# A state-space convolution beside a gathered expert layer: a half-width step tile, ScalarE's phase results written 128 bytes apart, one more slot for gathered rows

## The chip, the cores and the metric

The kernel runs on one core of a Trainium2 chip. The metric is the device time of one execution in microseconds (us). A core has five engines that run their own instruction queues and wait for each other through semaphores: PE multiplies matrices, DVE does elementwise work, ACT evaluates functions, POOL here mostly starts gathers, SP starts the plain DMAs. All DMAs share 16 DMA engines.

## The reference

The input `x` has 2048 rows of 448 numbers. It is normalised by row (`xn`), and three things are added: `x` itself, a state-space convolution of `xn` along the rows, and an expert layer on `xn`.

```
A = A_re + i A_im;  dt = exp(log_dt)
P = exp(dt * A * l)                      # l = 0 .. 2047, for 448 channels x 256 modes
K = real(sum over modes of C * P * dt*B) # one filter of 2048 taps per channel
y = conv(xn, K) + xn * Dskip             # by FFT in the reference
q = xn @ w_q;  s1 = q1 @ k1.T;  s2 = q2 @ k2.T     # 16 heads, 64 scores each
e = argmax(s1) * 64 + argmax(s2)                    # one of 4096 experts per head
out = sum over heads of gelu(xn . u[e]) * v[e]
result = x + y + out
```

The gate `g` is a softmax over one element.

## The kernel before

**Filter.** The 448 channels are taken in 56 batches of 8, with 2 x 128 modes a batch. Complex powers of each mode are built from a magnitude and a phase. The phase is an integer, of which the full range is one turn, so that it wraps by itself. On each of 128 partitions a batch has 32 phases (exponents) for each of 32 columns, which are its 8 channels for two halves of the modes and two base steps `h`; the names call a column a mode `m`. They are built for two batches at a time in `s.ph`, by doubling. The first row is copied from the loaded phases (`row(-1)`), and four adds (`row(0)` to `row(3)`, L614) double the number of rows, 1, 2, 4, 8, to 16; each adds a step that is the base step shifted left. The shifted steps of four batches lie in the step tile `st`, made by `sh` in `steps` with two shifts (L547), one per half `h`; there are 14 such tiles. In this version a row holds each phase for two neighbouring exponents `x` side by side, so the step tile holds each step twice. The integer add is a custom DVE instruction and appears in the profile as CUSTOM_DVE_ANT_0 on halves of 16 bits.

ScalarE then reads the phases through the view `four`: `trig` (L629) takes the sine, `trig2` (L632) the absolute value, and `trig3` (L635) the sine of a quarter turn less that, which is the cosine. The result `CS` is ordered by mode, and within a mode by the 32 exponents. `four` reads two neighbouring integers, then jumps 512 bytes; the writes are one run. DVE multiplies magnitude `mg` by `CS` (L660 to L666, tile `zi` and `mg`), PE sums over modes (`kp`, L682) and transforms (`vp`, L702), and ACT evicts to `VK` (L706).

**Convolution.** The channels are cut in chunks of 128, 128, 128 and 64. For each chunk PE transforms (`U`, L798 or L779), DVE multiplies (L808 or L786), PE transforms back (`ip`), the result goes through DRAM (`t_d`), and `final` makes the last transform and adds the rows to the output by an accumulating DMA on POOL (L1167).

**Experts.** `combine` multiplies keys and query weights once (`wc`, L862), so that the scores are one product per tile of 128 rows (L961, L970). DVE finds the two winners, their numbers `ig` go through DRAM, and for each of 16 tiles and 4 groups POOL starts 4 indirect gathers of 128 rows of 3584 bytes (L1083, 256 in all), a row being `u` and `v` of an expert. DVE takes the dot product (L1091), ACT and DVE make the gelu, PE sums with a masked weight (L1121), and the tile is added to the output (L1136).

**Slots.** Gathered rows, the loaded rows `xx`, the combined weights `W` and the convolution's big tiles share one pool of slots of 4 KB per partition: `UE` + 4 + 7 + 3, with `UE` = 11. A gather waits until the slot that it is given has been read for the last time. POOL's DMA descriptors have an area of 4096 bytes of each partition.

**Order.** The kernel is written as steps in some fifty streams (a stream is one kind of step, such as gathers or phase adds). The string `ORDER` names, character by character, the stream whose next step comes; it sets the sequence of every engine's instructions and the sequence in which slots are taken and given back. Waits between engines follow from what a step reads and writes. `Plan.run` checks that no step comes ahead of what it needs.

Of the kernel before, what the change touches and what calls it, by code (L numbers as in the profile page):

```python
# [85 lines left out]
def dv(n, k=1.0):  # L86
    return (66 + n / k) / 0.96
# [28 lines left out]
class Plan:  # L116
# [61 lines left out]
    "zUIygU!#ISh!h#yyyISRzKRVROizWx$W$%yyfziHHhNgxSfSzxPxKLISiz!#JM#RjRLRSfI!$$%QzIhhgTJfiIziGISSzMfykI!#yIyU#RUi&hRhh!yI$S$i"
    "dIeRXUSzUO%jhSIUNSlizIIhPkhLRhQzISMLhTMyRdiLzibURe!yyRzMfUzlyUiU##NY!U$$%LShSgJRjyRZZSifMhKhgHzz!UzKxiHfSfaN#Ufyy(LJ!Skh"
    "M#$hOPgUzxUiSL$%RRSyhhyymzxHTMhmlizxUUSRhhhn!nhHjhkhgLMURiUSLhhUyz#gRyRQV1iziSIiNI!fiIzz!ifSYclmISfhM#fQ$I$%hnSSgO#IyTWf"  # L180
    "IiUzjhiKZPhHI!&hRmUIhR#QkW$UhnI$UyyyyUzIzlzU%!hHjRy#z!iziS#Iy$RS$hkJyyyL%ZiUSzzHHdMhyRyLMelIbROzISz!I#!Iy#$SygiPfIhiSSXm"
    "zfzhRJmRUfRU$%L!nITnjhgfi#SIUIfMLhIhMkUIUiSgRRR#h!ISli$$N%OIJjKxcNJhzxyyVhhcyyxSzzSyUySUxzSzh!TPi#h!h#QmULUWZ$aih&Kyyhnf"
    "$UfURfU%MRziSzUgyzyLhNMhRgifSLfRQz!hSiH(yhg#HWzz#h!$R$hhbjZzz%Riyh!k#y!#MHYO$SSd$%iyHPIhekSizIIUSzlliIiRRLjhIKQghTzIUiSh"
    "UIR!#UihISMkhKyIyyfI!UI#URlmyS$I$fURfSShnJVY%NcgROhKxhfSajXxUizzyyPiSxzgLkhyymRQixzz!M#z#N!$Rhym$lhzfinyL&%RTSyzy(njUSUz"
    "hUz!yhhgzhzMU#Uhk!!SWR##il$$fh!Ri%R#hzhJfyi$yzfyxz$OzyfgxSxxS%KfimSiSiUhhP!gL#RMRhjhL#TiUiyUWSd!z$hRUSyzRMR$yy%yhkhSiyhS"
    "izUnjzhkilSROUNY(Qzlh!zhSzUPy&#!y#ymiSR$z$egyUb%hny!h#!aRyzTizfzUgzSfyyRURSXfiUR#$NQSU$UROzUihSSxoz!xYhgmzSf%yzSyP#h#Uy!"
    "h!hyfURRjnhTiRkhhS$U#hyS$y%UiymjUzilk!#UlxV$$xg%&hzzz!zzWh#!(Sn#hRSyyzyiz!iyyRmRS#V#$Wh!my$$inno$fUoyfigSSph%hzfgp%zfzUq"
    "rzqzyyphYj!hhzUrizfiyTkqpqroz#rhhhi#!!dpjqlW#$hrebiUh#kst$!hpg%pqWhxh$iorfoo$qltUxpgypyfzrhqxhciXfUg%irszijhUyifq&pzfrUi"
    "yhkhyyxy(zlzU!thozy#p#!qzz$hy$pjq!hr##iy!z$cay%yhhiyg$yUzfyUhzfqhrzhkpz%qr!pyyygUVzrtWihhuqppl#zfzyghrfi#!hy!ms(#fd#$yqm"
    "hyu!hr$%nqteth$ii$irnyiymjYbxxmhxsihnkxKnhjii%tzhWilgfhhYt&ykzgzzQffzzzz!yhhgh#if#yy!l$fmmh!$#h#!izz%iji$ynhyyuhnhyzkhhl"  # L190
    "z$zzihjgfhzi!hf#z!kayfli#gfifib$ih!hg$mhhuhijd%#hi)heh)(ym!nini#*ki$ljhxzXm%i+hhkf$xzxlxngh%hmgyyyizzifi&f!ynhhjgyy#yyhh"
    "i!khflf#zh$h*$y+hjmnkhca%hzziiilmnYyzg!hiz#y!hhzzyf#$zjgh$chzfykg%yh!zfzfifihdhzl#!hmi#i!eh##nh)o*+jb$i$!i$hg$ihk,%%ix)x"
    "lhhyh*zfmjx+niiyYygykhhyzff,aiyyyzyilgyxy,,yXyzzf!h&zhjmyfklgnz#o#h!zmyhy!n$$p#p!#hhhhqzhq$%zih$izpzizifr%jqprzhpgqrifzf"
    "ypqkhrfhrifqpYrcgh!hhsploihqh#ijritq#!ztk!rhpphqis#olxhbr$iq$frtptpd%qiz#fi!qehghpjhigkx$rqhuayr$xph%fgzyy(qyxyYfliurpzp"
    "zrhsfyhqh!hqhhrmttum#!ijhrhisi#nknhghhyziyyz$zz!$fyizf&fgtht%mhlzf#!i#giynhhmjhknfi$izdehhhzlmn!$huhjghhhykb(yg#yyy)iii#"
    "!%zfxzzfzx!$$al#h!hgfxy#ymyhyhifinchjx)*%yi$ykfiijhh$khh%z+hhlgizlzzhhyiim!nzzzi)yfizf#f#iy!$igjh(yyyy!&hg$fh%#hyk!*ydiz"
    "zlzz#f$$zzzzhmn*+hyhhh,+hbhiijykmni%e!gfilh)xfxo*hgi+f#i!!hihi##!$jg#ff$$,hxz$chkh%lzhyh%hyxzjaoYgizik!iilhyz#y,yyyhfyjh"
    "z#zfh!hgyzk!i$f$lym#y#h!y,yyyymnhgif$iz$hhnmdzizfjzzhnhemkhzzlizhbiixh&%yh!nhi#i!gh!hm%g#iniijhh(#j!fy#kf$k$fxlghhm%xfyh"
    "z$fl$oxhm%nnhhzpqhgp&pyy(yzziihz!rqiihqyzpr#!h#ajhqpi$f$zi%gyfrzhopq!rf#h#frgph!hzfiz$qhkrspl$%hqiripyzhhtqhyy(yytzbjgrq"
    "ziyphsqhhhzfyrfgpi!ktpthhyyyfgrqqi#uxypfrh!hzhyqprszfqho!ihi#ii$$hl#jthzhr!#if$rut%kpfjlgvhhxfiihgpqhfxh$igq%khrifrohxou"  # L200
    "ihhimjhiskowhtyltnhmvjnihizlzihviizimvjnm&ki!klnmijl#wzzww#nyyyzy!mkm$lz$zmn%nnpy!upp#yyyzyr)rs!z*tr#rzt$p$s+!rzzr#z)*#z"
    "!r!ttsu)$r%+#!tts$tt#(*%+,)$u$%,,&uu)*(+,*+)*,))**+++,,,")


class Kernel:
    OPT = dict(UE=11, XX=4, CS=2, ZI=2, MG=4, KT=4, HL=2, SG=1, XR=4, OB=3, XT=1, ST=1)

    def __init__(s, tc, es, io, **opt):
# [66 lines left out]
    def consts(s):  # L275
# [6 lines left out]
        def sets():  # L282
# [948 lines left out]
```

## Time and profile before

| | |
|---|---|
| median of 3 runs | 761.42 us (760.34 to 763.97) |
| the profiled execution, its own time | 763.02 us |
| its span, first to last instruction | 761.1 us (1.9 us lie around it) |
| busy in the span | DVE 669.5, PE 652.1, ACT 552.9, POOL 360.7 us |
| mean granted TensorE clock | 0.915 |
| DMA | 211.83 MB, 281 GB/s over the span |

In the groups of instructions a line reads: source line, engine, operation, output<-input, shapes, count; then busy time in us and mean ns of one; then the idle time of the engine ahead of them and who ended it. In the table by stretch each engine has its busy time and, in brackets, its instructions.

### The profile page before, as it was taken

How to read it: one execution, taken by the hardware profiler on the slowest of the kernel's cores; microseconds unless marked ns; L12 is line 12 of the kernel's file. 1: busy time of each engine (PE TensorE's matmuls, PEld its weight loads, DVE VectorE, ACT ScalarE, POOL GpSimd, SP SyncE). 2: the span in 40 equal slices, each digit the busy share in tenths (PEclk: the TensorE clock that was granted, in tenths of full speed). 3: DMA queues.
4: the chain of work that ended last, by engine and by line, in shares of the span. 5: the costliest groups of instructions: out<-in, count | busy, mean ns of one | idle time of the engine just before them, and what ended most of it. 6: DMA issues, size and time to landing. Idle time of an engine off the chain costs nothing.

```text
span 761.1 us, 19861 instructions
## 1 busy us (share of the span) xinstructions
PE 652.1 (86%) x7628; PEld 355.8 (47%) x7628; DVE 669.5 (88%) x1691; ACT 552.9 (73%) x1137; POOL 360.7 (47%) x307
## 2 busy tenths in 40 slices
PE   1999999999999999999887958679996587899882
PEld 0344333443444444444465734346763344576751
DVE  4896578999999999999999999999998999999840
ACT  3886147566876886774796898888898888999630
POOL 2011024544363645655447686484564657752523
PEclk9999999999999999999999877688987756999995
DMA  9998656978687896887989999899898999977998
GB/s 324 328 374 305 228 136 254 355 238 246 221 257 266 252 327 191 309 255 257 337 300 340 281 324 361 263 327 279 265 342 271 308 325 286 339 248 209 296 178 128
DMA packets 119095, 211.83 MB, mean 278 GB/s; under 512 B 38937, under 2 KB 94233, under 8 KB 118937
## 3 DMA queue, kind: packets, MB, share of 16 engines
q0 software_dynamic: 31232, 124.80, 51.6%
q1 hardware_dynamic: 87768, 85.77, 35.2%
q8 instruction: 60, 0.98, 0.5%
q14 instruction: 35, 0.28, 0.1%
HBM read 180.90 MB, written 33.29 MB: 281 GB/s over the span
## 4 chain that ended last, share of the span: by engine, by line
PE 41%; DVE 29%; ACT 14%; DMA 7%; issue 6%; SPq 1%; POOL 1%; POOLq 0%; DVEq 0%; ACTq 0%
PE sc L961 14%; DVE ue L1091 6%; PE U L798 3%; PE po L1121 3%; DVE mg L666 3%; DVE zi L662 3%; DVE ph L614 3%; PE kp L682 3%; PE sc L970 3%; DMA ue<-in_uv_dram,ig 3%; PE ip L830 2%; PE wc L862 2%; PE up L724 2%; ACT CS L629 2%; DMA VU<-vu_d 2%
## 5 line engine op out<-in xcount | busy, mean ns | idle before, releaser
L1083 POOL DMA_INDIRECT ue<-in_uv_dram,ig x256 | 312.6, 1221 | 309.0 <-PE po L1121 72.9
L961 PE MATMUL sc<-W,xt 128*128 128x512 f32 x384 | 180.1, 608 | 2.2 <-ACT xt L946 1.9
L1091 DVE SCALAR_TENSOR_TENSOR ue<-ue,xr 128x448 f32<-128x448 f32 x256 | 154.1, 617 | 4.0 <-DMA ue<-in_uv_dram,ig 4.0
L961 PEld LDWEIGHTS sc<-W,xt 128*128 128x128 f32 x384 | 69.7, 191 | 91.9 <-issue 83.9
L1121 PE MATMUL po<-ue,A 128*32 128x448 f32 x512 | 68.6, 616 | 9.4 <-DVE A L1114 5.0
L590 ACT ACTIVATE mg<-lg 128x512 f32<-128x512 f32 x112 | 63.4, 600 | 11.1 <-PE lg L579 10.6
L682 PE MATMUL kp<-mg 128*32 128x64 f32 x1792 | 62.3, 237 | 7.9 <-DVE kt L693 3.1
L666 DVE TENSOR_TENSOR mg<-mg,CS 128x1024 f32<-128x1024 f32 x56 | 68.2, 1217 | 0.0
L662 DVE TENSOR_TENSOR zi<-mg,CS 128x1024 f32<-128x1024 f32 x56 | 68.2, 1217 | 0.0
L635 ACT ACTIVATE CS<-CS,halfpi 128x1024 f32<-128x1024 f32 x56 | 64.5, 1152 | 0.8
L614 DVE CUSTOM_DVE_ANT_0 ph<-st,ph 128x512 uint16<-128x512 uint16 (+2 forms) x84 | 64.9, 772 | 0.2
L629 ACT ACTIVATE CS<-ph 128x1024 f32<-128x1024 int32 x56 | 62.6, 1118 | 1.4 <-issue 0.5
L632 ACT ACTIVATE CS<-ph 128x1024 f32<-128x1024 int32 x56 | 63.2, 1128 | 0.0
L682 PE MATMUL kp<-zi 128*32 128x64 f32 x1792 | 61.6, 234 | 0.0
L682 PEld LDWEIGHTS kp<-mg 128*32 128x32 f32 x1792 | 45.2, 119 | 29.2 <-issue 11.7
L579 PE MATMUL lg<-lc,rt 32*128 32x512 f32 x112 | 39.8, 548 | 21.5 <-ACT mg L590 17.5
L702 PE MATMUL vp<-f,kt 128*64 128x128 f32 x448 | 43.6, 326 | 16.5 <-ACT tl L1163 5.0
L985 DVE TENSOR_REDUCE mx<-sc 128x8 f32<-128x512 f32 x64 | 43.6, 682 | 14.6 <-PE sc L970 9.2
L682 PEld LDWEIGHTS kp<-zi 128*32 128x32 f32 x1792 | 47.2, 121 | 0.1
L798 PE MATMUL U<-VU,g 128*64 128x128 f32 x384 | 42.3, 301 | 5.4 <-DVE cp L808 2.7
L702 PEld LDWEIGHTS vp<-f,kt 128*64 128x64 f32 x448 | 28.9, 160 | 38.3 <-issue 11.9
L862 PE MATMUL wc<-wq,kk 128*64 128x448 f32 x128 | 31.7, 586 | 17.1 <-DMA wq<-in_wq_dram 17.1
(244 smaller groups left out, 1242.2 us busy)
## 6 DMA issues: line engine op xcount, KB each, us to landing
wq<-in_wq_dram SPq DMA_DIRECT2D x32, 448.0 KB
xr<-xn_d SPq DMA_DIRECT2D x64, 224.0 KB
vu_d<-vst SPq DMA_DIRECT2D x64, 112.0 KB
VU<-vu_d SPq DMA_DIRECT2D x12, 512.0 KB
t_d<-tq SPq DMA_DIRECT2D x24, 256.0 KB
tl<-t_d SPq DMA_DIRECT2D x12, 512.0 KB
ue<-in_uv_dram,ig POOLq DMA_INDIRECT x256, 6.4
xx<-in_x_dram SPq DMA_DIRECT2D x16, 224.0 KB
```

Of the source, the lines that this page charges most:

```text
L614: s.nc.vector.tensor_tensor(out=rw(n, 2 * n), in0=rw(0, n), in1=o["st"][:, k, b0:b0 + 2].rearrange("p b h m x -> p (b h m x)")[:, None].to ...
L629: s.nc.scalar.activation(CS[:, 1].rearrange("p (m r x) -> p m r x", r=16, x=2), four(s.ph), AF.Sin, scale=SC)
L635: s.nc.scalar.activation(B["CS"][:, 0], B["CS"][:, 0], AF.Sin, scale=-SC, bias=s.halfpi)
L662: V.tensor_tensor(out=zi[:, 512:], in0=mg[:, 512:], in1=CS[:, 1], op=ALU.mult)
L666: V.tensor_tensor(out=mg[:, 512:], in0=mg[:, 512:], in1=CS[:, 0], op=ALU.mult)
L682: s.nc.tensor.matmul(kp[32 * c:32 * c + 32, 64 * gi:64 * gi + 64], T[ri][:, 1024 + m:1056 + m], view(T[ri], m, [[512, 2], [1, 32]]), start ...
L702: s.nc.tensor.matmul(vp[64 * ri:64 * ri + 64, 128 * gi:128 * gi + 128], B["kt"][:, 64 * gi:64 * gi + 64], s.f1[:, ri], start=True, stop=True)
L798: s.nc.tensor.matmul(U[64 * h:64 * h + 64, sl, ri], s.g[q][:, 2 * kk + h, ri], src[:, k1 + h, :w], start=True, stop=True)
L961: s.nc.tensor.matmul(B["sc", q].rearrange("p a b -> p (a b)"), B["xt"][:, i], w, start=(q % 2 == 0 and i == 0), stop=(q % 2 == 1 and i == 2))
L1083: s.nc.gpsimd.indirect_dma_start(out=ue, out_offset=None, in_=s.io["uv"], in_offset=bass.IndirectOffsetOnAxis(ap=s.IDX[t][:, c, g:g + 1].b ...
L1091: s.nc.vector.scalar_tensor_tensor(Q["ue", c][:, :D], Q["ue", c][:, :D], 1.0, B["xr", c], op0=ALU.mult, op1=ALU.mult, accum_out=Q["dot"][: ...
L1121: s.nc.tensor.matmul(B["po"][32 * c:32 * c + 32, :D], Q["A"][:, c], Q["ue", c][:, D:], start=(g == 0), stop=(g == 3))
```

## The change

The step tile loses its repeat: `st` is half as wide, and each of its 28 shifts writes 256 integers, not 512. Phases of two neighbouring exponents no longer lie side by side. `s.ph` now has 32 rows of 64 phases, and the four adds double 2, 4, 8, 16 rows. The view `four` reads two neighbouring modes, then jumps 256 bytes, and since `CS` keeps its order by mode, the two results go to places 128 bytes apart. The shift amounts `amt` are stored the other way round. The first-row copy runs once per exponent, not once per half; both forms are two instructions of 64 elements.

`UE` becomes 12, and the descriptor area 2048 bytes. The string `ORDER` is another one from its first characters on, so nearly every engine's sequence differs.

```
-    "4HH4HH44441444Z4444H606HH414144114H72III2II72II2I2I7728I8I2IJJ22I2I2I2I72KIZ414I82852I24K4I4COP224C4234LMLDHMHHH4LMDCLM4"
+    "4HH4HH7474441464447I22II26442242I42IIC2447I1I4DI44012IC2I4I781HHJ414OECDC85FHH2JD8P274E8E4FLID7IIMF7IC2D22I4I44IECLCMID7"
...
-    OPT = dict(UE=11, XX=4, CS=2, ZI=2, MG=4, KT=4, HL=2, SG=1, XR=4, OB=3, XT=1, ST=1)
+    OPT = dict(UE=12, XX=4, CS=2, ZI=2, MG=4, KT=4, HL=2, SG=1, XR=4, OB=3, XT=1, ST=1)
...
-        s.ph = c.tile([128, 16, 2, 2, M, 2], I32, name="ph")
+        s.ph = c.tile([128, 16, 2, 2, 2 * M], I32, name="ph")
...
-            o["st"] = s.sm.tile([128, 4, 4, 2, M, 2], I32, name="st", bufs=s.o["ST"])
+            o["st"] = s.sm.tile([128, 4, 4, 2, M], I32, name="st", bufs=s.o["ST"])
             for h in range(2):
-                a = s.amt[:, h]
-                s.nc.vector.tensor_tensor(out=view(o["st"], 2 * M * h, [[16 * M, 4], [4 * M, 4], [1, 2 * M]]),
-                                          in0=view(o["tp"][:, 0, 0], 0, [[0, 4], [1, 4 * M], [0, 2]]),
-                                          in1=view(a, 0, [[1, 4], [0, 8 * M]]), op=ALU.logical_shift_left)
+                s.nc.vector.tensor_tensor(out=o["st"][:, :, :, h], in0=view(o["tp"][:, 0, 0], 0, [[0, 4], [M, 4], [1, M]]),
+                                          in1=view(s.amt, h, [[2, 4], [0, 4], [0, M]]), op=ALU.logical_shift_left)
...
-                    n = 1 << k
-                    s.nc.vector.tensor_tensor(out=rw(n, 2 * n), in0=rw(0, n),
-                                              in1=o["st"][:, k, b0:b0 + 2].rearrange("p b h m x -> p (b h m x)")[:, None].to_broadcast([128, n, 4 * R]),
-                                              op=ALU.add)
+                    n = 2 << k
+                    s.nc.vector.tensor_tensor(out=ph[:, n:2 * n], in0=ph[:, :n],
+                                              in1=o["st"][:, k, b0:b0 + 2].rearrange("p b h m -> p (b h m)")[:, None].to_broadcast([128, n, 2 * R]), op=ALU.add)
...
-            return view(v.rearrange("p r b h m x -> p (r b h m x)"), 2 * R * (b % 2), [[2, R], [4 * R, 16], [1, 2]])
+            return view(v.rearrange("p r x b m -> p (r x b m)"), R * (b % 2), [[2, M], [2 * R, 32], [1, 2]])
...
-            s.nc.scalar.activation(CS[:, 1].rearrange("p (m r x) -> p m r x", r=16, x=2), four(s.ph), AF.Sin, scale=SC)
+            s.nc.scalar.activation(CS[:, 1].rearrange("p (m c a) -> p m a c", a=32, c=2), four(s.ph), AF.Sin, scale=SC)
...
-            s.nc.scalar.activation(B["CS"][:, 0].rearrange("p (m r x) -> p m r x", r=16, x=2), four(s.ph), AF.Abs)
+            s.nc.scalar.activation(B["CS"][:, 0].rearrange("p (m c a) -> p m a c", a=32, c=2), four(s.ph), AF.Abs)
...
-    nc = bacc.Bacc("TRN2", target_bir_lowering=False, num_devices=1, dynamic_dma_scratch_size=4096)
+    nc = bacc.Bacc("TRN2", target_bir_lowering=False, num_devices=1, dynamic_dma_scratch_size=2048)
```

The first place is the start of SP's queue, which begins all plain loads. `pv` and `xx` are parameters and input rows, `kk` the keys, `wq` a head's weights for one side (PE's first product needs two of them), `lcf` a table for the magnitudes. Before:

```order
8 L419 DMA pv<-in_A_re_dram 128x896
9 L892 DMA xx<-in_x_dram 128x448 x3
10 L309 DMA kk<-in_k_dram 128x2x64 x2
11 L272 DMA ident<-in_ident_dram 128x128
12 L855 DMA wq<-in_wq_dram 128x896
13 L323 DMA lcf<-in_lc_dram 128x768
14 L855 DMA wq<-in_wq_dram 128x896
15 L327 DMA wtf<-in_wt_dram 128x64
```

And in the changed kernel:

```order
8 L419 DMA pv<-in_A_re_dram 128x896
9 L888 DMA xx<-in_x_dram 128x448 x2
10 L309 DMA kk<-in_k_dram 128x2x64 x2
11 L272 DMA ident<-in_ident_dram 128x128
12 L851 DMA wq<-in_wq_dram 128x896 x4
13 L323 DMA lcf<-in_lc_dram 128x768
14 L851 DMA wq<-in_wq_dram 128x896 x3
15 L327 DMA wtf<-in_wt_dram 128x64
```

The second `wq` load moved ahead of `lcf`, and one load of `xx` fewer stands in front of it.

The second place is on DVE, at the ninth of the 14 step tiles, about two thirds through its queue: `st` is the step tile, `ph` the phases, `mg`, `zi` and `CS` magnitude, product and sine, `ue` gathered rows, `kt` the filter piece. Before:

```order
925 L666 TENSOR_TENSOR mg<-mg,CS 128x1024
926 L1101 SCALAR_TENSOR_TENSOR x_5432<-x_5432,dot 128x4
927 L1110 TENSOR_TENSOR dw<-dot,ig 128x4
928 L547 TENSOR_TENSOR st<-tpl,amt 128x16x32 x2
929 L1107 SCALAR_TENSOR_TENSOR th<-th,dw 128x4
930 L660 SCALAR_TENSOR_TENSOR zi<-mg,CS 128x512
931 L1114 TENSOR_TENSOR A<-mask,th 128x128
932 L662 TENSOR_TENSOR zi<-mg,CS 128x1024
```

And in the changed kernel:

```order
924 L1087 SCALAR_TENSOR_TENSOR ue,dot<-ue,xr 128x448
925 L611 ISA ph<-st,ph 128x2048
926 L1097 SCALAR_TENSOR_TENSOR x_5312<-x_5312,dot 128x4
927 L546 TENSOR_TENSOR st<-tpl,amt 128x16x16 x2
928 L1106 TENSOR_TENSOR dw<-dot,ig 128x4
929 L1087 SCALAR_TENSOR_TENSOR ue,dot<-ue,xr 128x448 x2
930 L689 TENSOR_TENSOR kt<-kp,dsk 128x2
931 L656 SCALAR_TENSOR_TENSOR zi<-mg,CS 128x512
```

The two shifts stand at the same place in the queue and write half as much (16 x 16, were 16 x 32); what stands around them has changed places with other steps.

More of the change, by code (lines that the diff above doesn't have):

```diff
@@ L178 @@
[L178 to L189, printed above, removed]
```

60 lines of the change are left out of this document (36 added, 24 removed).

## The prediction

> **What bounds the kernel now.** The page's first two parts come first: who is busy, and when.
>
> ```profile
> PE 652.1 (86%) x7628; PEld 355.8 (47%) x7628; DVE 669.5 (88%) x1691; ACT 552.9 (73%) x1137; POOL 360.7 (47%) x307
> ...
> PE   1999999999999999999887958679996587899882
> PEld 0344333443444444444465734346763344576751
> DVE  4896578999999999999999999999998999999840
> ACT  3886147566876886774796898888898888999630
> ```
>
> DVE has the most work and stands at 9 from about 130 us to the last 40 us. PE stands at 9 too, but only up to about 320 us. So I cut the span there and asked for the busy times of each engine by stretch (columns: PE, PEld, DVE, ACT, POOL, then granted clock, DMA share, GB/s); the row of the first 20 us is from a finer cut.
>
> ```profile
> 0.00:20.00 20.00, 2.89 (x6) 0.81 (x7) 10.41 (x25) 8.40 (x19) 4.77 (x17) 1.00 0.89 318
> ...
> 0.00:140.00 140.00, 119.06 (x421) 47.31 (x422) 101.31 (x212) 79.64 (x199) 29.61 (x37) 1.00 0.80 280
> 140.00:320.00 180.00, 178.57 (x1416) 77.84 (x1415) 175.38 (x478) 131.26 (x293) 88.58 (x74) 1.00 0.80 262
> 320.00:720.00 400.00, 332.36 (x5347) 214.24 (x5346) 383.15 (x972) 334.38 (x627) 231.33 (x188) 0.86 0.93 297
> 720.00:762.00 42.00, 22.09 (x451) 16.40 (x450) 9.62 (x31) 7.63 (x21) 11.20 (x9) 0.75 0.86 157
> ```
>
> From 320 to 720 us DVE works 383 of 400 us and alone sets the pace: it idles 17 us, PE 68, ACT 66. From 140 to 320 us PE is full (1.4 us idle) and DVE nearly so (4.6 us). Before 140 us DVE idles 39 us behind the loads and PE. The chain of waits agrees: the scores on PE lead it, then DVE's lines.
>
> ```profile
> PE 41%; DVE 29%; ACT 14%; DMA 7%; issue 6%; SPq 1%; POOL 1%; POOLq 0%; DVEq 0%; ACTq 0%
> ```
>
> So DVE time saved after 320 us counts in full, and before 320 us in part.
>
> **The change part by part.** *The step tile.* The 14 step tiles take two shifts each, of 512 elements now and 256 after. Groups by line with shapes kept apart give the price; the last row group is the line of these shifts by stretch.
>
> ```profile
> L547 DVE TENSOR_TENSOR st<-tpl,amt 128x512 int32<-128x512 int32 x28 | 18.0, 682 | 0.0
> L664 DVE TENSOR_TENSOR mg<-mg,CS 128x512 f32<-128x512 f32 x56 | 38.3, 683 | 0.0
> L666 DVE TENSOR_TENSOR mg<-mg,CS 128x1024 f32<-128x1024 f32 x56 | 68.2, 1217 | 0.0
> ...
> 0.00:140.00 140.00, 1.28 (x2) 1.00 0.80 280
> 140.00:320.00 180.00, 3.85 (x6) 1.00 0.80 262
> 320.00:720.00 400.00, 12.84 (x20) 0.86 0.93 297
> ```
>
> A shift costs what a float operation of 512 costs (682 against 683 ns), and 512 elements more cost 534 ns, so 256 fewer save 267 ns and a shift takes about 415. Over 28 that is 7.5 us: 5.3 for the 20 after 320 us, 2.1 for the 8 before. The 5.3 count in full. Of the 2.1 I take half, 1.1, since PE is full there (bounds 0 and 2.1). The cover behind DVE after 320 us is wide, 66 us of ACT idle and 68 of PE.
>
> *The adds and the copy on DVE.* The four adds of a pair of batches still write 128, 256, 512 and 1024 integers (the page counts them as 16-bit halves); only the repeat of the second operand is shorter.
>
> ```profile
> L614 DVE CUSTOM_DVE_ANT_0 ph<-ph,st 128x256 uint16<-128x256 uint16 x28 | 7.9, 282 | 0.0
> L614 DVE CUSTOM_DVE_ANT_0 ph<-st,ph 128x512 uint16<-128x512 uint16 x28 | 11.7, 418 | 0.1
> L614 DVE CUSTOM_DVE_ANT_0 ph<-st,ph 128x2048 uint16<-128x2048 uint16 x28 | 34.0, 1215 | 0.0
> ```
>
> The first of these repeats nothing, the second twice, the last eight times, and all lie on one line (282 to 418 for 128 integers, 418 to 1215 for 768: 1.06 and 1.04 ns each). A repeat costs nothing, so I cost the adds at 0, and the first-row copy, 2 x 64 elements before and after, too.
>
> *ScalarE's phase reads.* Two passes per batch (Sin and Abs, 112 in all) still read pairs of neighbours, now 256 bytes apart and not 512; their results go in turns to two places 128 bytes apart, where they were one run. No row shows ACT writing single elements apart. The nearest rows:
>
> ```profile
> L629 ACT ACTIVATE CS<-ph 128x1024 f32<-128x1024 int32 x56 | 62.6, 1118 | 1.4 <-issue 0.5 <-DVE ph L614 0.4 <-DVE mg L666 0.2
> L632 ACT ACTIVATE CS<-ph 128x1024 f32<-128x1024 int32 x56 | 63.2, 1128 | 0.0
> L450 ACT ACTIVATE pw<-pv 128x896 f32<-128x896 f32 x1 | 0.9, 949 | 0.0
> L706 ACT ACTIVATE VK<-vp 128x256 f32<-128x256 f32 x56 | 21.5, 387 | 13.4 <-PE vp L702 13.3
> L803 ACT ACTIVATE us<-U 128x256 f32<-128x256 f32 x48 | 18.3, 388 | 6.7 <-PE U L798 5.9 <-DVE cp L808 0.8
> L837 ACT ACTIVATE tq<-ip 128x512 f32<-128x512 f32 x24 | 13.9, 600 | 2.1 <-PE ip L830 2.1
> ```
>
> L706 writes runs of 8 elements, 512 bytes apart, and reads PSUM with every element 128 bytes from the last, at 387 ns; L803, all in one run, takes 388. By this row the new write is free. The other end: L803 and L837 give 0.83 ns an element, so a pass of 1024 in one run would take 949 + 128 x 0.83 = 1055 ns; the pair reads take 63 to 73 ns more for 512 jumps, 0.13 ns a jump. Charged for each of 1024 written elements that is 0.13 us a pass, 15 us on ACT. ACT holds 14% of the chain, so 2.1 us of it would reach the end. Below nothing: if the shorter jump freed the reads of their 70 ns, 7.8 us of ACT, 1.1 us of the end. I take +1.0, the middle of 0 and 2.1.
>
> The Trainium skill's page SBUF — State Buffer (Specifications, and the note on SBUF cachelines) speaks against this write: lines are 16 bytes, full speed needs at least two hits on a line, and every change of line pays. It gives no figure; L706's runs change line every fourth element at no cost. If the rule bites in the new pattern, the sum goes the way of the first rival below.
>
> *The start.* Both programs begin with the same loads, in another order on SP.
>
> ```profile
> PE wc L862 <- DMA wq<-in_wq_dram: 17.1, 2, 16.4
> ...
> xx<-in_x_dram SPq DMA_DIRECT2D x16, 224.0 KB
> lcf<-in_lc_dram SPq DMA_DIRECT2D x1, 384.0 KB
> ```
>
> PE's first product waits 16.4 us for its second weight load. One row load of 224 KB and the 384 KB of lcf now stand behind that load: 608 KB at the 318 GB/s of the first 20 us are 2.0 us. PE is full soon after, so its start can move the end; but its later weights, evictions and scores are reordered too, and I take half, 1.0 (bounds 0 and 2.0).
>
> *Slots and descriptor area.* Counting along the written order, the shared ring of 25 slots runs empty in the old order; in the new one, of 26, four are always free. A gather then takes a slot freed longer ago, and POOL can run ahead.
>
> ```profile
> DVE ue L1091 <- DMA ue<-in_uv_dram,ig: 4.0, 3, 2.0
> ...
> POOL ue L1083 <- PE po L1121: 72.9, 23, 9.5
> ...
> ue<-in_uv_dram,ig POOLq DMA_INDIRECT x256, 6.4
> ```
>
> POOL waits 73 us for slots, yet DVE waits for gathered rows only 4.0 us: all that earlier gathers can bring is 4.0. I take 0. Nothing in the trace shows the descriptor area. A gather lands in 6.4 us; 256 in the 600 us between the first and the last are 2.7 in flight on average, and halving room for them is costed at 0 (bound: POOL's own 1% of the chain, 8 us).
>
> The Trainium skill's page DMA: Bandwidth & Descriptors (Terms; Why a DMA increments its semaphore by 16 and not by 1) has descriptors of 16 bytes and 16 engines; by it, as an estimate, 2048 bytes are 128 descriptors an engine, 9 a gather with its completion, so 14 gathers, more than the 12 slots.
>
> *The rest of the order.* Every engine's sequence is written anew. The instructions of each engine keep their number, but for ACT, which gets two more table loads (64, were 62).
>
> ```profile
> L590 ACT ACT_TABLE_LOAD x26 | 33.4, 1283 | 0.5
> ```
>
> That is 2.6 us of ACT and, at its 14% of the chain, 0.4 at the end. Otherwise only waits can come or go: DVE's 17 us of idle after 320 us is all that a better order could remove there, and a worse one can add as much. I take 0 for these, and widen the range.
>
> *Sum.* 763.0 us, the profiled execution, less 5.3, 1.1 and 1.0, plus 1.0 and 0.4: 757.0. That execution lies 1.6 us above the median of the three runs, 761.4, which is what the result is held against; in its terms the sum is 755.4.
>
> **The rivals.** *The scattered write costs a second cycle.* With 0.83 ns more on each of 1024 elements a pass takes 0.85 us longer, 95 us over 112. Three quarters of the passes lie after 320 us (42 of the 56 of L629):
>
> ```profile
> 320.00:720.00 400.00, 47.01 (x42) 0.86 0.93 297
> ```
>
> ACT there goes from 334 to 405 us, above DVE's 378; with DVE's present 4% of idle the stretch takes 423, 23 us more. Before 320 us 24 us fall on an engine that is idle for a third; 14% of them, 3, reach the end. With the start's gain: 763 + 23 + 3 - 1 = 788 profiled, 786 in the median's terms. It decides from about 0.5 us a pass, where ACT reaches DVE's 378; below that the 14% hold. Against it stand L706 and the reads, which pay 70 ns and no more.
>
> *The saving turns into a wait.* After 320 us DVE waits elsewhere for what it no longer works: PE runs at a granted clock of 0.86 and hands to ACT and back for each batch. Then 5.3 and 1.1 are lost and the start's 1.0 and ACT's 1.0 cancel, and the table loads' 0.4 stay: 763.4 profiled, 762 in the median's terms. For it speaks that DVE, 88% busy, holds only 29% of the chain; against it, the 66 us and more that ACT and PE idle there.
>
> *The new order adds idle.* If POOL's lead crowds SP's loads (DMA is busy 0.93 after 320 us), DVE's idle there could rise by half, 8.5 us, and eat more than the 6.4 saved: 757.0 + 8.5 = 765.5 profiled, 764 in the median's terms; if by all 17 us, 772.
>
> *The new order is better.* DVE's 4.0 us of gather waits and the start's and the early shifts' other halves come in as well: 763.0 - 7.5 - 2.0 - 4.0 = 749.5, in the median's terms 748.
>
> **How the numbers follow.** The sum holds with 0.52, the better order 0.07, the saving lost 0.18, the slow write 0.15, more idle 0.08. A measurement of this kernel tells about 0.5%, 3.8 us, from no change: faster is below 757.6, slower above 765.2. The forecast spreads by its unknown costs from 751 to 759, and a little of it falls within; the milder shades of the slow write and of the added idle lie above 765. So faster 0.57, same 0.19, slower 0.24. The range goes from 747, just past the better order, up to 778, which takes in the milder slow writes and leaves out most of the full one (0.12) and a little below (0.04).
>
> **What would show it.** Right: L547's successor at about 415 ns x28; DVE's busy sum near 662 us; the passes of Sin and Abs within 1055 to 1190 ns; PE's first product at about 14.5 us; DVE's idle after 320 us still near 17 us. The slow write would show as passes near 1.97 us and DVE waiting for CS; the lost saving as DVE idle grown by 5 us or more with the new releaser named; crowding as DVE or PE waiting for xr, VU or ue. The prediction is wrong if the passes take over 1.6 us, or if DVE's busy sum falls as said and the time does not.

## The result: 14 per cent slower, and the profile after

| | before | after |
|---|---|---|
| median | 762.69 us (4 runs, 760.34 to 765.49) | 868.41 us (4 runs, 866.06 to 871.74) |
| ratio | | 1.139 (95%: 1.133 to 1.145) |
| profiled span | 761.1 us | 864.3 us |

Predicted were 755.4 us, 747 to 778. The result lies 105.7 us above the kernel before, and on the side to which 0.24 was given. Executions have a faster and a slower state, and all medians and ratios below are of the faster ones.

The page of the changed kernel, busy times, slices and the chain that ended last:

```profile
PE 684.8 (79%) x7628; PEld 374.8 (43%) x7628; DVE 665.0 (77%) x1691; ACT 651.3 (75%) x1139; POOL 336.4 (39%) x307
...
DVE  5565988987877998998888787878878788987610
ACT  2757377877868867857878899988989899999420
...
ACT 46%; PE 33%; DVE 10%; issue 6%; DMA 4%; POOL 1%; SPq 1%; POOLq 0%; ACTq 0%; DVEq 0%
ACT CS L625 11%; ACT CS L628 10%; PE sc L957 10%; ACT CS L631 4%; PE ip L826 3%; ACT L635 3%; PE kp L678 3%; PE po L1117 3%; PE lg L577 2%; ACT mg L588 2%; ACT mg L590 2%; DVE ue L1087 2%; PE sc L966 2%; ACT L588 1%; PE lg L579 1%
```

DVE's work went down as said (669.5 to 665.0 us), but its row in the slices is no longer a row of nines. ACT has 98 us more work (552.9 to 651.3) and its share of the chain went from 14 to 46%, led by the two phase passes, L625 and L628. The groups by line show why, with the step tile's shifts below them:

```profile
L628 ACT ACTIVATE CS<-ph 128x1024 f32<-128x1024 int32 x56 | 115.5, 2063 | 0.0
L625 ACT ACTIVATE CS<-ph 128x1024 f32<-128x1024 int32 x56 | 115.5, 2062 | 0.0
...
L631 ACT ACTIVATE CS<-CS,halfpi 128x1024 f32<-128x1024 f32 x56 | 64.4, 1149 | 1.0
...
L546 DVE TENSOR_TENSOR st<-tpl,amt 128x256 int32<-128x256 int32 x28 | 10.5, 417 | 0.0
```

A pass of Sin or Abs takes 2062 ns where it took 1118 and 1128; the cosine pass L631, which writes in one run, stayed as it was (1152 before). The shift takes 417 ns, predicted 415. DVE's waits and two stretches:

```profile
DVE x L1097 <- ACT x L1094: 28.1, 17, 7.3
DVE kt L689 <- ACT kt L686: 24.5, 13, 3.6
DVE th L1103 <- ACT th L1100: 20.1, 17, 3.3
DVE ph L607 <- ACT CS L628: 17.8, 9, 3.2
...
140.00:320.00 180.00, 164.39 (x1264) 70.28 (x1266) 152.76 (x432) 135.85 (x261) 72.46 (x63) 0.96 0.75 236
320.00:720.00 400.00, 306.30 (x4148) 185.44 (x4144) 333.09 (x857) 341.03 (x534) 195.12 (x173) 0.81 0.84 263
```

DVE's idle time from 320 to 720 us is 67 us (17 before). Most of its waits are not for CS: they are for short steps of ACT (`x`, `th`, `kt`), 73 us. Laid beside ACT's own timeline, ACT is in one of the two long passes for 25 of these 73 us, and in other steps or itself waiting for the rest. One such case (start, duration; in brackets the idle time ahead and who ended it):

```profile
642.56 1.97 ACT L628 ACTIVATE CS<-ph 128x1024 f32<-128x1024 int32 x1
644.34 0.30 ACT L686 ACTIVATE kt<-kp 128x126 f32<-128x126 f32 x1
644.67 0.16 DVE L689 TENSOR_TENSOR kt<-kp,dsk 128x2 f32<-128x2 f32 x1 [3.58 <-ACT kt L686]
```

No wait for gathered rows is left.

The end changed too. POOL's last stores, in the same columns, before and after:

```profile
747.18 1.28 POOL L1167 DMA_DIRECT2D out_dram<-tl  x1 [1.83 <-ACT tl L1163]
749.16 1.27 POOL L1167 DMA_DIRECT2D out_dram<-tl  x1 [0.70 <-ACT tl L1163]
754.16 1.27 POOL L1167 DMA_DIRECT2D out_dram<-tl  x1 [3.73 <-ACT tl L1163]
756.01 1.29 POOL L1167 DMA_DIRECT2D out_dram<-tl  x1 [0.57 <-ACT tl L1163]
```

```profile
851.06 1.29 POOL L1163 DMA_DIRECT2D out_dram<-tl  x1 [2.78 <-issue]
855.07 1.28 POOL L1163 DMA_DIRECT2D out_dram<-tl  x1 [2.71 <-issue]
859.19 1.29 POOL L1163 DMA_DIRECT2D out_dram<-tl  x1 [2.84 <-issue]
```

Before, ACT's last eviction ends at 755.6 us, and the program 5.5 us later. After, it ends at 847.75 and the program 16.6 us later: POOL issues its stores one every 4.0 to 4.1 us, though their data has long been there.

### The profile page after: what moved, and what is told of

It is laid out like the page before. It is cut to its first block, busy times and chain, and to the rows that moved or that the text cites. A ratio compares the mean times of both kernels' runs of the same rounds, so it can differ in the third digit from the quotient of the medians.

```text
span 864.3 us, 19854 instructions
## 1 busy us (share of the span) xinstructions
PE 684.8 (79%) x7628; PEld 374.8 (43%) x7628; DVE 665.0 (77%) x1691; ACT 651.3 (75%) x1139; POOL 336.4 (39%) x307
## 4 chain that ended last, share of the span: by engine, by line
ACT 46%; PE 33%; DVE 10%; issue 6%; DMA 4%; POOL 1%; SPq 1%; POOLq 0%; ACTq 0%; DVEq 0%
ACT CS L625 11%; ACT CS L628 10%; PE sc L957 10%; ACT CS L631 4%; PE ip L826 3%; ACT L635 3%; PE kp L678 3%; PE po L1117 3%; PE lg L577 2%; ACT mg L588 2%; ACT mg L590 2%; DVE ue L1087 2%; PE sc L966 2%; ACT L588 1%; PE lg L579 1%
## 5 line engine op out<-in xcount | busy, mean ns | idle before, releaser
L1079 POOL DMA_INDIRECT ue<-in_uv_dram,ig x256 | 288.0, 1125 | 362.7 <-PE po L1117 170.2
L628 ACT ACTIVATE CS<-ph 128x1024 f32<-128x1024 int32 x56 | 115.5, 2063 | 0.0
L625 ACT ACTIVATE CS<-ph 128x1024 f32<-128x1024 int32 x56 | 115.5, 2062 | 0.0
L1117 PE MATMUL po<-ue,A 128*32 128x448 f32 x512 | 71.4, 633 | 15.6 <-DVE A L1110 13.4
L577 PE MATMUL lg<-lc,rt 32*128 32x512 f32 x112 | 44.8, 591 | 45.0 <-ACT VK L702 18.8
L678 PE MATMUL kp<-mg 128*32 128x64 f32 x1792 | 68.3, 249 | 9.1 <-DVE mg L662 3.0
L611 DVE CUSTOM_DVE_ANT_0 ph<-st,ph 128x256 uint16<-128x256 uint16 (+1 forms) x112 | 72.9, 651 | 0.4
L678 PE MATMUL kp<-zi 128*32 128x64 f32 x1792 | 67.9, 247 | 0.0
L631 ACT ACTIVATE CS<-CS,halfpi 128x1024 f32<-128x1024 f32 x56 | 64.4, 1149 | 1.0
L678 PEld LDWEIGHTS kp<-mg 128*32 128x32 f32 x1792 | 49.4, 127 | 31.4 <-issue 11.4
L826 PE MATMUL ip<-cp,e 64*128 64x256 f32 x384 | 53.9, 433 | 3.3 <-ACT tq L833 2.2
L577 PEld LDWEIGHTS lg<-lc,rt 32*128 32x128 f32 x112 | 17.6, 214 | 79.6 <-ACT VK L702 23.4
L678 PEld LDWEIGHTS kp<-zi 128*32 128x32 f32 x1792 | 51.3, 129 | 0.2
```

The source lines that it names most:

```text
L577: s.nc.tensor.matmul(ps, ro["rt"][rs, i], s.lc[rs, :512], start=True, stop=True)
L625: s.nc.scalar.activation(CS[:, 1].rearrange("p (m c a) -> p m a c", a=32, c=2), four(s.ph), AF.Sin, scale=SC)
L628: s.nc.scalar.activation(B["CS"][:, 0].rearrange("p (m c a) -> p m a c", a=32, c=2), four(s.ph), AF.Abs)
L631: s.nc.scalar.activation(B["CS"][:, 0], B["CS"][:, 0], AF.Sin, scale=-SC, bias=s.halfpi)
L678: s.nc.tensor.matmul(kp[32 * c:32 * c + 32, 64 * gi:64 * gi + 64], T[ri][:, 1024 + m:1056 + m], view(T[ri], m, [[512, 2], [1, 32]]), start ...
L826: s.nc.tensor.matmul(Q["ip", h][:, 2 * w * x:2 * w * x + 2 * w], s.e[r, k], Q["c", x][r, :, ab, ri], start=(i == 0), stop=(i == 3))
```

## The experiments

They ran in five groups; the kernels of a group share a chip and the runs of the kernel before. In groups 1, 2 and 4 the kernel before takes 834 to 843 us and not 763. It isn't the chip, as the expectations on record took it to be: groups 2, 3 and 4 ran on the same one. The last section shows what differs; a result is compared only with others of its group. The table gives medians and, of the ratio to the kernel before of the same group, the 95% interval.

| group (before) | run | median us | ratio |
|---|---|---|---|
| 1 (839.4) | e3_one_run | 858.6 | 1.026 (1.017 to 1.035) |
| 1 | e4_old_apart | 883.6 (one run) | 1.05 |
| 1 | e5_sin_only | 880.7 | 1.049 (1.037 to 1.062) |
| 1 | e8_interleaved | 862.8 | 1.029 (1.023 to 1.036) |
| 2 (842.5) | e1_old_order | 917.9 | 1.093 (1.074 to 1.111) |
| 2 | e2_new_order | 853.6 | 1.012 (0.997 to 1.027) |
| 2 | e9_interleaved_old_order | 850.6 | 1.011 (1.000 to 1.023) |
| 3 (762.9) | f1_after | 870.1 | 1.144 (1.135 to 1.152) |
| 3 | f2_one_run | 793.6 | 1.040 (1.032 to 1.049) |
| 3 | f3_interleaved_old_order | 782.7 | 1.028 (1.020 to 1.036) |
| 3 | f4_one_run_slots11 | 778.1 | 1.022 (1.010 to 1.033) |
| 4 (834.1) | g1_area_only | 848.6 | 1.015 (1.004 to 1.025) |
| 4 | g2_tile_only | 833.3 | 1.000 (0.996 to 1.005) |
| 4 | g3_order_only | 849.3 | 1.018 (1.010 to 1.026) |
| 4 | g4_write_only | 895.8 | 1.078 (1.067 to 1.089) |
| 5 (763.6) | h1_old_start_new_rest | 778.7 | 1.021 (1.013 to 1.028) |
| 5 | h2_new_start_old_rest | 779.0 | 1.021 (1.013 to 1.029) |

### The scattered write

The theory (W) was that the write by turns doubles the pass, and that this is all. Its edit away, in e3 and again in f2 beside the changed kernel itself (f1):

```
-            s.nc.scalar.activation(CS[:, 1].rearrange("p (m c a) -> p m a c", a=32, c=2), four(s.ph), AF.Sin, scale=SC)
+            s.nc.scalar.activation(CS[:, 1].rearrange("p (m a c) -> p m a c", a=32, c=2), four(s.ph), AF.Sin, scale=SC)
(and the same for Abs; e5 does it for Abs alone)
```

> The changed kernel with everything kept (half-width step tile, order, 12 slots, descriptor area) except that the Sin and Abs passes write their 1024 results in one run. The modes of a pair then lie side by side in CS, where the products do not look for them, so the cosines and sines are used for the wrong modes; the work is otherwise the same. Theory W (the write by turns 128 bytes apart is the cause, and all of it): the two lines fall from 2062 ns to between 1120 and 1190 (the one-run write of before plus the reads in pairs), ACT loses about 100 us of busy time, and the kernel falls from 868 to 750-762 us. Rival R (the reads of the argument in pairs, not the writes, double the pass): the two lines stay near 2060 ns and the time stays at 860-870. Rival O (the other order or the slots and descriptor area cost most): the passes fall to 1.15 us, but the time stays above 800.

> The changed kernel with only the Sin pass writing by turns; the Abs pass writes in one run (so the cosines lie in the wrong places). Half the dose: ACT's added time is about 53 us in place of 105. Theory 1:1 (every added microsecond of a pass is handed on, because short ACT steps that others wait for stand behind the passes in ACT's queue): 806-820 us, about halfway between 757 and 868. Rival T (ACT's idle time soaks up the first part and only what is beyond a threshold reaches the end, as the prediction's 14 per cent or its cover of idle time had it): 765-785 us.

> The changed kernel itself, beside its one-run version on the same chip (the chips of the first two groups of runs took 840 to 844 us for the kernel before, not 762, so the changed kernel's 868 can't stand beside their results). Theory W with every microsecond handed on: 100 us or more over the one-run version of the same call. Theory W with part of it covered (half of Sin and Abs by turns cost 22 us of the 52 us that it added to ScalarE there): 40 to 65 us over it.

> The changed kernel with Sin and Abs writing in one run (the modes of a pair then lie where the products do not look for them), a second time, for the difference to the changed kernel on one chip. If this chip is like the first (before at 762): 752-765; if it is like the two since (before at 840): 850-862, 1 to 2.6% over the kernel before, by the order.

The two passes in f2, with half-width tile and pair reads kept:

```profile
L628 ACT ACTIVATE CS<-ph 128x1024 f32<-128x1024 int32 x56 | 62.7, 1119 | 0.0
L625 ACT ACTIVATE CS<-ph 128x1024 f32<-128x1024 int32 x56 | 62.6, 1119 | 0.4 <-DVE ph L611 0.2
```

1119 ns, so the write doubles the pass and the reads cost nothing: rival R falls. In group 3 the write alone is worth 870.1 - 793.6 = 76.5 us, for 112 x 0.94 = 105 us more of passes; it lies between the two cases of f1's expectation. "Every microsecond handed on" falls with that, though the first comparison (105 us more of passes, 105.7 us more of time) looks just like it. "A threshold" does not fall: half the dose (e5, two runs, 52 us more of passes) cost 22 us over e3, inside the 8 to 28 us that e5's expectation gives to rival T (765 to 785, from 757), and both doses lose about 30 us on the way (52 - 22 and 105 - 76.5). It is no threshold of sums, since ACT's 603 us of work in e5 are still 62 less than DVE's. The two doses ran in different groups, so how the price grows with the dose stays open. Where a part of it gets through, DVE's waits in f2 show:

```profile
DVE x L1097 <- ACT x L1094: 15.6, 9, 8.4
DVE th L1103 <- ACT th L1100: 12.3, 9, 2.5
DVE kt L689 <- ACT kt L686: 11.0, 11, 2.3
```

The same three waits for short steps of ACT come to 39 us where they were 73, and ACT is in one of the two passes for 4 of them where it was for 25. And W's "all of it" falls: f2 misses its 752 to 765 by 29 us.

The same write added alone to the kernel before, in e4 and g4:

```
-            s.nc.scalar.activation(CS[:, 1].rearrange("p (m r x) -> p m r x", r=16, x=2), four(s.ph), AF.Sin, scale=SC)
+            s.nc.scalar.activation(view(CS, 1024, [[64, 16], [16, 2], [1, 16], [32, 2]]), four(s.ph), AF.Sin, scale=SC)
(and the same for Abs; `four` gets a fourth dimension to match and reads in the same order)
```

> The kernel before, its order, slots and step tile kept, with one thing added: Sin and Abs write their results by turns 128 bytes apart (some values then lie in other places of CS, so the products use them for the wrong modes; the work is the same). Theory W: the two passes go from about 1.12 to 2.0-2.06 us, ACT gains about 100 us, and the kernel goes from 762 to 850-870 us without any other part of the change. Rival O: the passes double, but the time stays below 800 us, since before's order or its eleven slots leave room that the new order does not. Rival R (reads, not writes): passes stay near 1.12 us and the time at 762.

> The kernel before with Sin and Abs writing by turns 128 bytes apart (some values lie in other places of CS), all else as before. Theory W, 1:1: 100 to 108 us slower. Theory W with cover: 70 to 80 us, as the changed kernel stands over its one-run version (76), if neither order hides more than the other; under 60 if before's order has more room.

The passes went to 2050 to 2066 ns in both, and the time up by 62 us in g4 (44 in the one run of e4). e1 and e9 below differ in little but the write, in the order of before: 67 us. In these groups PE idles more (last section); that this is why less of the write reaches the end is not shown.

What a pass pays for was measured by itself:

```
+ for _ in range(8): nc.scalar.activation(view(w, OUT), view(a, IN), AF.Abs)      # 17 ways, each on a line of its own
+ for _ in range(8): nc.vector.tensor_tensor(out=view(v, OUT), in0=view(a, IN), in1=view(b, IN), op=ALU.mult)   # 4 ways
```

> The write by itself: 8 passes of ScalarE (Abs, 128x1024, float32) and of VectorE (a product, 128x1024) for each way of reading and writing, each on a line of its own, with nothing beside them but one transfer at the start; it computes nothing of the reference. Theory W (an element that does not follow its neighbour in the same short stretch of memory costs ScalarE a second cycle): one run 1.0-1.12 us; by turns 128 or 64 bytes apart 1.95-2.06 us; singles 128 bytes on 1.95-2.06 us; runs of 8 (32 bytes) 1.0-1.15 us; reads at any stride 1.0-1.2 us. Rival (the cost is of the alternation, back and forth, not of the jump): by turns 2 us, singles 128 bytes on 1.0-1.2 us. What 8, 12 and 16 bytes cost is open: if the stretch is 16 bytes, singles 16 bytes on cost 2 us and singles 8 bytes on 1.0-1.5 us.

The groups by line, in the order of the source: ACT writing in one run (L32), by turns 16 (L36) and 128 bytes apart (L40), in runs of two elements 128 bytes on (L42), single elements 8 (L48), 16 (L52) and 128 bytes on (L54); reading single elements 8 (L56) and 16 bytes on (L58) and pairs 256 bytes on (L62); then DVE in one run (L66), writing by turns 128 bytes apart (L68) and reading singles 128 bytes on (L72).

```profile
L32 ACT ACTIVATE w<-a 128x1024 f32<-128x1024 f32 x8 | 8.5, 1057 | 2.3 <-DVE w L29 2.1
L36 ACT ACTIVATE w<-a 128x1024 f32<-128x1024 f32 x8 | 16.5, 2065 | 0.3
L40 ACT ACTIVATE w<-a 128x1024 f32<-128x1024 f32 x8 | 16.1, 2009 | 0.3
L42 ACT ACTIVATE w<-a 128x1024 f32<-128x1024 f32 x8 | 8.6, 1075 | 0.3
L48 ACT ACTIVATE w<-a 128x1024 f32<-128x1024 f32 x8 | 8.9, 1116 | 0.3
L52 ACT ACTIVATE w<-a 128x1024 f32<-128x1024 f32 x8 | 16.0, 1998 | 0.3
L54 ACT ACTIVATE w<-a 128x1024 f32<-128x1024 f32 x8 | 15.5, 1932 | 0.3
L56 ACT ACTIVATE w<-a 128x1024 f32<-128x1024 f32 x8 | 9.0, 1122 | 0.3
L58 ACT ACTIVATE w<-a 128x1024 f32<-128x1024 f32 x8 | 16.1, 2013 | 0.3
L62 ACT ACTIVATE w<-a 128x1024 f32<-128x1024 f32 x8 | 8.5, 1062 | 0.3
L66 DVE TENSOR_TENSOR v<-a,b 128x1024 f32<-128x1024 f32 x8 | 9.8, 1225 | 0.3
L68 DVE TENSOR_TENSOR v<-a,b 128x1024 f32<-128x1024 f32 x8 | 15.9, 1991 | 0.3
L72 DVE TENSOR_TENSOR v<-a,b 128x1024 f32<-128x1024 f32 x8 | 17.0, 2129 | 0.3
```

On ACT 1024 elements take 1056 to 1122 ns where each shares its 16 bytes with the element just before or just after it, and 1932 to 2065 where none does; how far the jump goes beyond that makes little difference, nor does it matter whether it goes back and forth. Reads pay as writes do, which no theory had, and so does DVE. The Trainium skill's page SBUF — State Buffer (Specifications, and the note on SBUF cachelines) says that full bandwidth needs two hits or more on a line of 16 bytes; ACT's rows agree in each of the 17 ways. That each cross to a new line costs something, as it says too, they do not show where a line gets its two hits: runs of two (L42) take 18 ns more than one run, runs of four and eight nothing. The price here is 0.85 to 0.98 ns on ACT and 0.70 to 0.88 ns on DVE for each element that stands alone.

### The area for descriptors

f2 left 31 us over the kernel before. The first edit against that:

```
-    OPT = dict(UE=12, XX=4, ...
+    OPT = dict(UE=11, XX=4, ...
-    nc = bacc.Bacc("TRN2", target_bir_lowering=False, num_devices=1, dynamic_dma_scratch_size=2048)
+    nc = bacc.Bacc("TRN2", target_bir_lowering=False, num_devices=1, dynamic_dma_scratch_size=4096)
```

> The one-run version with 11 slots for gathered rows and 4096 bytes for descriptors, as before. The replay of the order never leaves fewer than four slots free, so the slots should change nothing: within 1% of the one-run version in this call. If the smaller descriptor area makes gathers wait, this is faster by 4 to 10 us and the idle time of VectorE before the gathered rows falls.

It is 15.5 us faster than f2, more than the 4 to 10 us expected, and at the end, not at the gathers. Its last stores, and then those of g1, which adds the 2048 bytes alone to the kernel before:

```profile
762.65 1.27 POOL L1163 DMA_DIRECT2D out_dram<-tl  x1 [0.77 <-ACT tl L1159]
765.51 1.27 POOL L1163 DMA_DIRECT2D out_dram<-tl  x1 [1.59 <-issue]
768.25 1.29 POOL L1163 DMA_DIRECT2D out_dram<-tl  x1 [1.46 <-ACT tl L1159]
```

> The kernel before with one edit: 2048 bytes for POOL's descriptors in place of 4096. Theory D (a store of results needs so much of the smaller area that the next one waits until it has landed): the last stores of POOL are issued 4.0 us apart, as in the profiles of all versions with 2048 bytes, not 1.3 to 2.7; the time from the last product to the end goes from 6 to 18 us, and the kernel is 10 to 15 us slower, 1.3 to 2%. Rival (the twelfth slot or the order does that): within 0.5% of the kernel before.

```profile
833.41 1.29 POOL L1167 DMA_DIRECT2D out_dram<-tl  x1 [2.78 <-issue]
837.40 1.28 POOL L1167 DMA_DIRECT2D out_dram<-tl  x1 [2.70 <-issue]
841.55 1.29 POOL L1167 DMA_DIRECT2D out_dram<-tl  x1 [2.86 <-issue]
```

In f4 a store follows the last one after 2.9 and 2.7 us, and two earlier ones 1.3 us apart; with 2048 bytes each is issued 4.0 to 4.2 us after the one ahead. In g1 the DMA engines move a store's data until 832.8, 836.7 and 840.9 us, and the next store is issued 0.6 to 0.7 us after that each time; in f4 the last is issued at 768.25, while the one ahead moves data until 768.9. From ACT's last eviction to the end are 5.5 to 5.7 us in before, f4, g2, g3 and g4, 19.2 in f2, 18.5 in g1, and 14 to 19 in all ten profiles with 2048 bytes. g1 is 12 to 15 us slower than the kernel before (by the ratio and by the medians; the interval is wide, 3 to 21), and its end is 13 us longer: theory D holds, and the twelfth slot isn't needed to explain it. No run changes the slot alone.

### The step tile without the write

If the columns of the position table are laid out so that the modes of a pair lie side by side, the passes write one run, and PE reads every second element:

```
-                lc[:, kind, c, 256 * half + 32 * c + a] = bj[32 * half + a]
+                lc[:, kind, c, 256 * half + 64 * (c // 2) + 2 * a + c % 2] = bj[32 * half + a]
...
-                            s.nc.tensor.matmul(kp[...], T[ri][:, 1024 + m:1056 + m], view(T[ri], m, [[512, 2], [1, 32]]), ...)
+                            s.nc.tensor.matmul(kp[...], view(T[ri], 1024 + m, [[2, 32]]), view(T[ri], m, [[512, 2], [2, 32]]), ...)
```

e8 has this with the new order, e9 and f3 with the order of before, all three with 12 slots and 2048 bytes; g2 has the order, slots and area of before, and so the tile alone.

> A version meant to keep the half-width step tile without the write by turns: the columns of the position table are laid out with the two modes of a pair side by side, so that mg, zi and CS all hold them so, Sin and Abs write in one run, and TensorE's products for the kernels read their 32 columns at every second element. Theory W: the passes are near 1.12-1.19 us, and the time is 750-762 us if TensorE's reads at a stride of 8 bytes cost nothing. Rival S (those reads are slower): the 896 small products of that line and their weight loads grow; if each took twice as long on a path that the chain runs through, 770-790 us.

> Half-width step tile, pairs of modes stored side by side so that Sin and Abs write in one run, TensorE's small products reading at every second element, and before's written order. Step tile's saving alone: 5 to 8 us under the kernel before (ratio 0.990 to 0.994). If the new order was what kept the same version with it 2.9% over the kernel before, this one falls to a ratio of 0.985 to 1.005; if TensorE's strided reads, the half-width tile or the slots did that, it stays at 1.02 to 1.035.

> Half-width step tile, pairs of modes side by side, one-run writes, TensorE reading at every second element, before's order: the candidate to beat both. Where before takes 762: 752-758 (the step tile's 7.5 us of VectorE). Where before takes 840: 0.995 to 1.02 of it, VectorE's saved time being covered there by TensorE's longer stretches.

> The half-width step tile alone: modes of a pair side by side, one-run writes, TensorE reading at every second element, before's order, 11 slots and 4096 bytes. By the prediction's step for the tile (7.5 us of VectorE, 6.4 of them at the end) 754 to 760 where the kernel before takes 762 to 765, a ratio of 0.988 to 0.995. The same with 12 slots and 2048 bytes stood at 1.028; if the descriptor area takes 13 to 15 us of that, this one comes to 1.008 to 1.011, and the half-width tile then brings nothing, or TensorE's reads at a stride cost what it brings.

e8 stands with e3 (862.8 and 858.6), so PE's reads at a stride cost little, if anything. f3 is 20 us slower than the kernel before, of which its end (18.4 us from the last eviction, not 5.5) explains 13; the other 7 are open. g2 is the version that should have beaten both kernels: DVE's work is down (670.7 us in g1, 664.0 in g2), and the time is that of the kernel before, 1.000 (0.996 to 1.005), between the two cases that its expectation sets apart, as e9's is. g2 ran only in group 4, where the kernel before takes 834 us; where it takes 763, the tile alone was not run. Nothing here beats the kernel before.

### The order

```
-    "4HH4HH44441444Z4444H606HH414144114H72III2II72II2I2I...
+    "4HH4HH7474441464447I22II26442242I42IIC2447I1I4DI440...   (all 29 lines; e1 the other way round)
```

> The changed kernel with before's written order (half-width step tile, scattered writes, 12 slots and the descriptor area kept). Theory W (the scattered write is the cause, the order is not): within 3% of what the changed kernel takes on a chip where the kernel before takes 762, so 850-895 there; on a chip where before takes 840, 885-905. Rival O (the new order costs most of it): 765-800 where before takes 762.

> The kernel before (full step tile, one-run writes, 11 slots) with the changed kernel's written order. Theory W: the order is nearly neutral, within 1.5% of the kernel before on the same chip (where before takes 762: 752-774). Rival O (the new order adds idle time of its own; the one-run version of the changed kernel stayed 2.6% over the kernel before on the chip of its run): 2 to 4% over the kernel before (where before takes 762: 777-793).

> The kernel before with the changed kernel's written order, all else as before; on a chip where the kernel before took 844 it came to 1.012 (0.997 to 1.027). Theory O (the 14 us that stay in the one-run version with 11 slots and 4096 bytes are the order's): 1.012 to 1.022. Rival (they are the tile's or the reads'): 0.995 to 1.005.

e1 shows that the old order does not mend the rest (917.9, more than the 885 to 905 expected). e2 was too coarse to tell; g3, the same kernel again, gives 15 us, 1.8% (1.0 to 2.6%), and that is also what stays in f4 (15.2 us). Where it is lost, by the stretches of before and of f4 (columns as in the prediction):

```profile
0.00:240.00 240.00, 217.91 (x1220) 90.97 (x1220) 199.57 (x481) 150.46 (x361) 73.12 (x72) 1.00 0.80 272
240.00:720.00 480.00, 412.08 (x5959) 248.43 (x5960) 460.27 (x1180) 394.83 (x755) 276.39 (x226) 0.89 0.91 292
```

```profile
0.00:240.00 240.00, 208.94 (x1114) 86.50 (x1114) 183.75 (x443) 152.91 (x350) 67.25 (x68) 0.99 0.77 258
240.00:720.00 480.00, 404.35 (x5811) 240.18 (x5812) 459.57 (x1199) 389.61 (x753) 271.92 (x226) 0.92 0.92 292
```

DVE has done 15.8 us less work by 240 us and as much as before from there on: in f4 the new order loses at the start. DVE's two largest waits there that the kernel before does not have are 9.6 us for ACT's `xx` (L907) and 7.1 us for the load of `dt`; h2 below, which has the new start, has them too (9.8 and 6.8). Two kernels put one order's first 30% of DVE's steps in front of the other's rest:

```
+ ORDER = old[:1065] + (new less the steps already written)      # h1;  h2: new[:1064] + (old less those)
```

> The kernel before with its own order up to 30% of VectorE's work, and from there the changed kernel's order (less the steps already written). If the start loses the 15 us: within 0.6% of the kernel before. If the rest loses them: 1.2 to 2.2% over it.

> The reverse: the changed kernel's order up to 30% of VectorE's work, then the kernel before's. If the start loses the 15 us: 1.2 to 2.2% over the kernel before, VectorE having done about 16 us less work by 240 us. If the rest loses them: within 0.6% of the kernel before.

h2 came out as the start's guilt has it (1.021, and DVE at 185.1 us of work by 240 us). But h1, which should then be free of it, is as slow. A rest that was written to follow another start may lose by the seam, and these runs can't tell that from a loss of its own. That the order costs about 15 us is shown; that its start does it is what the traces of f4 and h2 say, and h1 speaks against it.

## Why the prediction was wrong

In group 3 the 107.2 us between f1 and the kernel before part into 76.5 for the write (f1 less f2), 15.5 for the area and the slot (f2 less f4) and 15.2 for order and tile (f4 less before). Both signs that the prediction named for being wrong came: passes over 1.6 us, and DVE's sum down without the time. By its steps:

- **ScalarE's phase reads: the step that failed.** "By this row the new write is free" took L706, runs of 8 elements, as the nearest row to single elements. Its runs change line every fourth element at no cost, that was read rightly, and e6 shows runs of two to be free as well (L42, 1075 ns). But no run of two or more says anything of a run of one. The other end, 0.13 us a pass, came from reads in pairs, which by e6 pay nothing for their jump (L62, 1062 against 1057 ns). Measured: 0.94 us a pass, 105 us of passes and 76.5 us of time, where the sum has +1.0 (0 to 2.1). The Trainium skill's page cited beside it spoke for this cost, and was set aside for L706.
- **The first rival had the pass right (1.97 us, measured 2.06) and the end wrong.** It gave the write 23 + 3 = 26 us; f1 less f2 is 76.5. It took DVE's idle share and ACT's sum as the measure: after 320 us ACT reaches the end only where its work exceeds DVE's. In the trace after, ACT is idle for a quarter of the span and still holds 46% of the chain: short steps that stand behind a pass in ACT's queue wait for it, and DVE waits in turn (25 us of the 73 are seen directly). "ACT holds 14% of the chain" was a share of the old chain, not the price of more work on ACT.
- **Descriptor area: 0 taken, 8 bound, 12 to 15 measured.** The step counted gathers, 2.7 in flight. It did not ask what else POOL issues. The four last stores are 128 KB each in pieces of 256 bytes, 32 an engine (the trace has 2112 packets for the four, 33 for each engine and store). With the Trainium skill's page DMA: Bandwidth & Descriptors (Terms, and The descriptor swizzle: one closing descriptor on each side) that is, as an estimate, 33 reads and 33 writes an engine. If reads and writes share the 128 places that the prediction works out for 2048 bytes, two stores need 132 and don't fit, and the pitch of 4 us, one store at a time, agrees; if each side has 128 of its own, as the prediction's 9 a gather has it, two would fit. No run here tells the two apart: that the area does it is shown, how its places are counted is not.
- **The order: 0 taken, 17 as the bound, about 15 measured.** The third rival (764 to 772) was right in sign and size; its reason was not what came: in f4 DVE waits 3.5 us for `xr` and not for gathered rows, and by 240 us it is 15.8 us behind. PE's second weight load did come earlier (15.6 us of waiting, 16.4 before: 0.8 of the 2.0 us); nothing of it is seen at the end.
- **The step tile: right in time, nothing at the end.** 417 ns for 415, and DVE's sum 665.0 for 662. But g2's 1.000 leaves no room for the 5.3 us that "count in full": in group 4 the second rival (the saving turns into a wait) is what happened. Where DVE sets the pace as in the first profile, no run has the tile alone; f3 and f4 show no gain there either.
- **The sum and the chances.** The rivals were weighed against each other, with 0.15, 0.18 and 0.08. But they hang on different edits, so one doesn't exclude another, and a part of each of the three came at once. Their times should have been added, not only their chances.

## What to carry to other kernels

When a view's innermost step leaves a 16-byte piece of memory with one 32-bit element read or written in it, price the pass at 0.7 to 1.0 ns more for each element (about twice the time on ACT, 1.6 to 1.7 times on DVE), reads and writes alike; keep pairs together on both sides. An engine that is a quarter idle still sets the end if short steps that others wait for stand in its queue behind long ones: ask what stands behind the instruction that grows, not how busy its engine is. And take each edit of a change as a risk of its own that adds to the others; a smaller area or a new order that looks free needs a look at everything that it touches, the last stores of the program too.

## What the runs showed of the hardware

In three of the five groups the kernel before ran in 834 to 843 us, in the others in 763 to 764, and on one and the same chip in either way. What differs in the traces is the time between PE's small products. The chain of waits around one batch of 64 products, in the first profile of the changed kernel and in e3 (group 1):

```profile
145.63 1.08 PE kp L678 x63
```

```profile
144.79 0.90 PE kp L678 x48
145.69 0.42 issue
146.11 0.32 PE kp L678 x4
146.43 0.41 issue
...
```

In e3 the first 48 products run at the same pace, and then they come in two fours and a seven with 0.4 us between, in which PE waits for nothing that the profile shows: 3.1 us in all for what took 1.1. By groups, in the kernel before and in g1, of group 4 (the products are the same):

```profile
L682 PE MATMUL kp<-zi 128*32 128x64 f32 x1792 | 61.6, 234 | 0.0
```

```profile
L682 PE MATMUL kp<-zi 128*32 128x64 f32 x1792 | 76.9, 234 | 18.7 <-issue 18.1 <-DMA ue<-in_uv_dram,ig 0.4
```

234 ns a product in both, and 18.7 us of idle time in place of none. In every profile of groups 1, 2 and 4 this line idles for 15 to 24 us, with either area, and in every other profile of the kernel for 0.0. It is a part of the 70 to 80 us; what PE waits for there, and why in some groups only, no run shows.
